# Small SBUF passes of VectorE moved to GpSimd and ScalarE, the first keys transposed by TensorE, and the stores issued from ScalarE

## The chip, the cores and the metric

The kernel runs on one core of one Trainium2 chip. The metric is the device time of one execution in microseconds, as the median of several runs. The core has five instruction streams: TensorE (PE, with its weight loads as PEld), VectorE (DVE), ScalarE (ACT), GpSimd (POOL) and SyncE (SP), which only issues DMAs here. Each stream runs in its own order and waits for the others by semaphores.

## The reference

Two layers follow one another. First an attention through 49 agents, with B = 4 batches of N = 11456 tokens of 128 channels:

```python
a2k = sm(agents, k)             # softmax over the tokens, 49 x N
agent_v = a2k @ v               # 49 x 128
q2a = sm(q, agents)             # softmax over the agents, N x 49
x = q2a @ agent_v               # N x 128
```

`sm` scales by 1/sqrt(128), subtracts the maximum, takes exp and divides by the sum. Then a mixture of 8 experts over all 45824 tokens, the best one for each:

```python
xn = x / (norm(x) + 1e-6); en = expert_emb / (norm(expert_emb) + 1e-6)
logits = xn @ en.T / tau
gate_w = softmax(logits)[argmax]
out[t] = gate_w * (relu(x[t] @ w1[e]) @ w2[e])      # e = argmax of token t, F = 1024
```

Inputs and output are fp32.

## The kernel before, in words

**Tiles.** A batch is cut into 12 units (`u`): eleven of 128 partitions x 8 token columns, and a last one of 96 x 2. Two tiles of 4 columns (512 tokens) make a unit; a batch has 23 tiles. Units are grouped for routing: group 0 is unit 0, and every later group two units.

**Stages of a batch.** (1) Key scores: each unit of `k` is transposed, multiplied with the agents, and a running maximum `m_run` is kept (`k1_unit`, `k1_f32`). (2) Value sums: `kd` = exp(scores - max), and `avp` = kd x v, added into `avx` (`k2_unit`). (3) `av_chain` divides, gives `avT`, and makes a small matrix `r_hi`, `r_lo` that yields in one product a token's logits, sum and quadratic form. (4) `pick_expert` guesses the batch's expert, loads its `w1` and `w2`, forms gh + gl = avT x w1 in two fp16 halves, and w2h + w2l. (5) Query units (`q_unit`): scores, exp, a split into `e` high and low halves, a transpose to `tt`, and the product `rtp` with r_hi, r_lo. (6) `route_group`: the gate `gs` of a group's tokens by some fifteen small passes over 128 x 16 or 128 x 16 x 8 numbers. (7) The expert steps: for each tile 8 steps of `ffn_mm1` (hp = gh x tt, L722 and L723, then ScalarE's relu `hh` L726 and VectorE's residual `hl` L727) and, four steps later, `ffn_mm2` (yp, L744 to L746); after eight steps `ffn_out` multiplies by the gate into `ot` (L759) and stores it (L765). There are 4 x 23 x 8 = 736 steps. (8) Tokens whose best expert is not the guessed one ("strays") are repaired in a late pass.

**fp16 split against fp32.** Most units are split into two fp16 halves (`split`: square and sum on ScalarE, a power-of-two scale in three tiny VectorE passes `half_scale`, the high half on ScalarE, the low half by two GpSimd passes L303 and L304), transposed by a DMA, and multiplied in three fp16 products. `pe_T` and `k1_f32` instead transpose in fp32 on TensorE (L364), copy the result out of PSUM (half on ScalarE, half on VectorE) and multiply in fp32 (L382). In the first batch the units 1, 3, 5 and 7 of `k` (`K16`) take a quick form of the split, with the low half on VectorE (L306) and the DMA transpose issued from ScalarE's queue (L309); the other eight are `k1_f32`.

**Order.** The program is written as generators that yield steps; `first` lists the work before the expert steps, with units of the next batch or of queries placed between the values by the table `BETWEEN`. During the expert steps `keys` spreads the next batch's units over the steps and `queries` starts each query unit some units ahead. A scheduler then orders each engine's instructions by a model of the machine; SyncE's order is kept as written in the first stage. PSUM has four banks for `hp`, two for `yp`, and two for scores and small products. Loads of k, q and v share eleven SBUF buffers (`ld`).

Until batch 0's gates' factor exists no expert step runs, so the program has a first stage (to the first L722) and then the expert stage, in which the next batch's keys and values and all queries run between the steps.

Of the kernel before, what the change touches and what calls it, by code (L numbers as in the profile page):

```python
# [30 lines left out]
def kernel(ctx: ExitStack, tc: tile.TileContext, q, k, v, agents, emb, tau, w1, w2, out):  # L31
# [141 lines left out]
    def half_scale(ssq, kexp, tag, bufs=2, fold=None):  # L173

        p = ssq.shape[0]
        sc = sm.tile([P, 1], F32, name="hsc", tag=tag + "c", bufs=bufs)[:p]
# [4 lines left out]
        dve.tensor_scalar(si, si, EXPONENT, None, ALU.bitwise_and)
        yield 1
        dve.tensor_scalar(iv.bitcast(I32), si, -1.0, float(254 * ONE), ALU.mult, ALU.add)
        if fold is not None:
            yield 1
            dve.tensor_scalar(iv, iv, fold[:p], None, ALU.mult)
# [104 lines left out]
    def split(kind, b, u, g, quick=False):  # L291
# [7 lines left out]
        hs = half_scale(sq, 14, kind + "u", 4, escale if kind == "q" else None)  # L299
        sc, iv = now_run(hs) if quick else (yield from hs)  # L300
        act.activation(xs[:p, :n, 0], s[:p, :n], AF.Copy, scale=sc)  # L301
        if not quick:
            pool.tensor_tensor(out=s[:p, :n], in0=s[:p, :n], in1=sc.unsqueeze(2).broadcast_to([p, n, D]), op=ALU.mult)  # L303
            pool.tensor_tensor(out=xs[:p, :n, 1], in0=s[:p, :n], in1=xs[:p, :n, 0], op=ALU.subtract)  # L304
# [4 lines left out]
        (act if quick else sp).dma_start_transpose(out=xT[:, : 2 * n, :p], in_=xs[:p, :n].rearrange("p c h d -> p (c h d)"))  # L309
# [62 lines left out]
    def k1_f32(b, u):  # L372
# [12 lines left out]
        act.activation(st, spv, AF.Copy, scale=sga[:p])  # L385
# [235 lines left out]
    def route_group(b, gi, n):  # L621
# [18 lines left out]

        pool.tensor_scalar(quad[:, :n], quad[:, :n], 1e-36, None, ALU.max)
# [1 line left out]
        dve.tensor_scalar(l.unsqueeze(2), rtg[:, :n, E:], 1e-9, None, ALU.add)
# [2 lines left out]
        pool.tensor_tensor(out=nrm, in0=quad[:, :n], in1=half[:, :n], op=ALU.pow)  # L646
# [21 lines left out]
        dve.scalar_tensor_tensor(out=el, in0=es, scalar=1e-9, in1=l, op0=ALU.add, op1=ALU.mult)  # L668
# [6 lines left out]
        dve.tensor_scalar(gs[:, :n], gs[:, :n], bt.iall, None, ALU.mult)  # L675
# [72 lines left out]
    def ffn_out(b, t):  # L748
# [16 lines left out]
        sp.dma_start(out=dst, in_=o[:p, :n])  # L765
# [364 lines left out]
```

## Time and profile before

| | |
|---|---|
| median of 3 runs | 1150.92 us (1150.88 to 1152.09) |
| the profiled execution | 1146.91 us, span 1145.1 us |
| first expert matmul (L722) | 121.84 us after the span's start |
| PE / DVE / ACT / POOL busy | 1031.5 / 866.8 / 712.7 / 515.4 us |
| mean granted TensorE clock | 0.947 |

Times are microseconds from the span's start. A row of the timeline is start, duration, engine, line, operation, output<-input, shapes and count, and in brackets how long the engine had idled and who released it. "SPq" and "ACTq" are DMA instructions on an engine's queue; they are not counted as busy. A row of the waits is: who waited for whom, the sum in us, how often, the longest. A row of the groups ends with busy us, mean ns of one | idle time before it and its releasers. The granted clock is the share of TensorE's full clock. Line numbers are those of the kernel before; in the changed one most are one or two off (L727 for L726, L728 for L727, L760 for L759, L766 for L765).

### The profile page before, as it was taken

What the parts mean: (1) busy time and instruction counts of PE and PEld (TensorE: products, weight loads), DVE (VectorE), ACT (ScalarE), POOL (GpSimd) and SP (SyncE); (2) the same over time, 40 slices, a digit from 0 to 9 for tenths busy, and PEclk for the clock granted to TensorE, in tenths of its full rate; (3) what the DMA queues carried; (4) which work ended last, traced back from release to release, by engine and by line L of the source; (5) the groups of instructions that cost most, each with busy time, mean ns of one, the idle gap of its engine ahead of it and who ended that gap; (6) DMA issues with size and microseconds to landing.
All of it is one profiled execution on the core that took longest, in us unless ns stands there. A gap on an engine that the chain in (4) does not pass through costs nothing.

```text
span 1145.1 us, 34081 instructions
## 1 busy us (share of the span) xinstructions
PE 1031.5 (90%) x13878; PEld 815.1 (71%) x13878; DVE 866.8 (76%) x2056; ACT 712.7 (62%) x1338; POOL 515.4 (45%) x449
## 2 busy tenths in 40 slices
PE   4677788999998888889999889999999799999997
PEld 4666566777777766667777667777778577887776
DVE  5446787877787778768688688877678889787785
ACT  4454967776657866756654876665455756655553
POOL 2262688756512986535430677354221624242100
PEclk9557899999999899999999899999999899999999
DMA  9959879953456997654433997733203534331100
GB/s 322 181 150 166 266 163 235 240 141 104 80 105 221 206 230 139 147 103 119 92 87 80 271 240 176 150 72 80 59 22 108 119 65 137 100 81 46 41 29 33
DMA packets 292264, 154.72 MB, mean 135 GB/s; under 512 B 216635, under 2 KB 268939, under 8 KB 292107
## 3 DMA queue, kind: packets, MB, share of 16 engines
q1 hardware_dynamic: 283723, 150.44, 54.9%
q10 hardware_dynamic: 8320, 2.10, 1.3%
q8 instruction: 109, 1.79, 0.6%
q14 instruction: 48, 0.39, 0.1%
q0 software_dynamic: 64, 0.00, 0.0%
HBM read 75.80 MB, written 23.53 MB: 87 GB/s over the span
## 4 chain that ended last, share of the span: by engine, by line
PE 53%; DMA 14%; issue 11%; DVE 9%; POOL 7%; ACT 4%; SPq 1%; ACTq 0%; POOLq 0%; DVEq 0%
PE hp L722 9%; PE yp L744 9%; PE yp L746 9%; PE yp L745 9%; PE hp L723 9%; PE avp L408 4%; DMA tt<-e 4%; DMA kt<-in_k_dram 3%; DVE hl L727 3%; DMA kT<-ks 2%; DMA qT<-qs 2%; POOL qt L303 2%; POOL kt L303 1%; POOL ks L304 1%; ACT hh L726 1%
## 5 line engine op out<-in xcount | busy, mean ns | idle before, releaser
L727 DVE SCALAR_TENSOR_TENSOR hl<-hp,hh 128x512 f16<-128x512 f32 (+1 forms) x736 | 479.6, 669 | 112.3 <-ACT hh L726 91.9
L726 ACT ACTIVATE hh<-hp 128x512 f16<-128x512 f32 (+1 forms) x736 | 416.5, 585 | 223.7 <-PE yp L745 132.4
L744 PE MATMUL yp<-w2h,hh 128*128 128x128 f16 (+1 forms) x2880 | 523.3, 220 | 6.4 <-ACT hh L726 6.2
L745 PE MATMUL yp<-w2l,hh 128*128 128x128 f16 (+1 forms) x2880 | 523.0, 220 | 2.7 <-DVE w2l L533 2.7
L746 PE MATMUL yp<-w2h,hl 128*128 128x128 f16 (+1 forms) x2880 | 522.4, 220 | 0.0
L744 PEld LDWEIGHTS <-hh 128*128 128x128 f16 (+1 forms) x2880 | 285.2, 99 | 61.5 <-ACT hh L726 8.5
L746 PEld LDWEIGHTS <-hl 128*128 128x128 f16 (+1 forms) x2880 | 285.6, 99 | 46.5 <-issue 3.9
L722 PE MATMUL hp<-tt,gh 128*128 128x512 f16 (+1 forms) x736 | 279.2, 379 | 40.0 <-DVE hl L727 35.3
L745 PEld LDWEIGHTS <-hh 128*128 128x128 f16 (+1 forms) x2880 | 285.2, 99 | 38.4 <-issue 0.3
L723 PE MATMUL hp<-tt,gl 128*128 128x512 f16 (+1 forms) x736 | 278.8, 379 | 0.0
L615 POOL TENSOR_TENSOR rt<-rt,qe 128x392 f32<-128x392 f32 (+1 forms) x48 | 46.3, 965 | 163.2 <-ACT rt L614 163.1
L303 POOL TENSOR_TENSOR qt<-qt,hsc 128x1024 f32<-128x1024 f32 (+1 forms) x46 | 81.9, 1783 | 66.2 <-ACT qs L301 52.8
L723 PEld LDWEIGHTS <-gl 128*128 128x128 f16 x736 | 72.5, 99 | 48.3 <-issue 46.3
L581 POOL TENSOR_TENSOR e<-qe,e 128x392 f16<-128x392 f32 (+1 forms) x48 | 41.5, 865 | 140.0 <-DVE e L580 62.9
L304 POOL TENSOR_TENSOR qs<-qt,qs 128x1024 f16<-128x1024 f32 (+1 forms) x46 | 93.1, 2027 | 0.6
L303 POOL TENSOR_TENSOR kt<-kt,hsc 128x1024 f32<-128x1024 f32 (+1 forms) x36 | 64.4, 1790 | 57.5 <-ACT ks L301 57.5
L722 PEld LDWEIGHTS <-gh 128*128 128x128 f16 x736 | 72.5, 98 | 10.0 <-issue 9.0
L304 POOL TENSOR_TENSOR ks<-kt,ks 128x1024 f16<-128x1024 f32 (+1 forms) x36 | 73.0, 2028 | 0.6
L759 DVE TENSOR_TENSOR ot<-yp,gs 128x512 f32<-128x512 f32 (+1 forms) x92 | 61.4, 668 | 14.5 <-PE yp L746 13.9
L646 POOL TENSOR_TENSOR nrm<-quad,half 128x16 f32<-128x16 f32 (+2 forms) x28 | 68.4, 2443 | 2.0
L408 PE MATMUL avp<-vt,kd 128*64 128x129 f32 x720 | 62.8, 298 | 5.1 <-ACT kd L402 4.8
L297 ACT ACTIVATE qs<-qt 128x1024 f16<-128x1024 f32 (+1 forms) x46 | 46.0, 1001 | 31.6 <-DMA qt<-in_q_dram 13.9
(258 smaller groups left out, 1483.7 us busy)
## 6 DMA issues: line engine op xcount, KB each, us to landing
kt<-in_k_dram SPq DMA_DIRECT2D x44, 512.0 KB, 6.0
qt<-in_q_dram SPq DMA_DIRECT2D x44, 512.0 KB, 7.0
vt<-in_v_dram SPq DMA_DIRECT2D x44, 512.0 KB, 5.4
out_dram<-ot SPq DMA_DIRECT2D x88, 256.0 KB, 2.2
w1s<-in_moe_w_dram SPq DMA_DIRECT2D x5, 512.0 KB, 3.6
w2s<-in_moe_w_dram SPq DMA_DIRECT2D x5, 512.0 KB, 4.9
qT<-qs SPq DMA_TRANSPOSE x46, 4.7
tt<-e SPq DMA_TRANSPOSE x46, 2.9
```

The lines of the kernel that those rows point to most:

```text
L303: pool.tensor_tensor(out=s[:p, :n], in0=s[:p, :n], in1=sc.unsqueeze(2).broadcast_to([p, n, D]), op=ALU.mult)
L304: pool.tensor_tensor(out=xs[:p, :n, 1], in0=s[:p, :n], in1=xs[:p, :n, 0], op=ALU.subtract)
L408: pe.matmul(out=avp[hs, :W], lhsT=de[:p, c * A : c * A + LO], rhs=src[:p, c, :], start=(c < 2), stop=(c >= n - 2), skip_group_check=True)
L646: pool.tensor_tensor(out=nrm, in0=quad[:, :n], in1=half[:, :n], op=ALU.pow)
L722: pe.matmul(out=hp[:, :m], lhsT=bt.gh[:, fs], rhs=tt, start=True, stop=False)
L723: pe.matmul(out=hp[:, :m], lhsT=bt.gl[:, fs], rhs=tt, start=False, stop=True)
L726: act.activation(hh[:, :m], hp[:, :m], AF.Relu)
L727: dve.scalar_tensor_tensor(out=hl[:, :m], in0=hp[:, :m], scalar=0.0, in1=hh[:, :m], op0=ALU.max, op1=ALU.subtract)
L744: pe.matmul(out=y, lhsT=hh[:, cs], rhs=bt.w2h[:, f, :], start=(f == 0 and c == 0), stop=False, skip_group_check=True)
L745: pe.matmul(out=y, lhsT=hh[:, cs], rhs=bt.w2l[:, f, :], start=False, stop=False, skip_group_check=True)
L746: pe.matmul(out=y, lhsT=hl[:, cs], rhs=bt.w2h[:, f, :], start=False, stop=last, skip_group_check=True)
L759: dve.tensor_tensor(out=o[:p, :n], in0=yp[:p, :n], in1=gate, op=ALU.mult)
```

## The change

Four things are changed.

1. All twelve units of batch 0's keys take `k1_f32`. The quick form of `split` is gone, and the scale of the scores is folded into the agents' power-of-two scale (`sga_s`). The table `BETWEEN` has four entries in place of seven: two query units and two key units of batch 1 (it had five keys).
2. In `route_group` the logits are no longer divided before their maximum is taken: the maximum is taken of the raw logits (`rmx`), subtracted, and then scaled. Additions, products and the subtraction go to GpSimd; the two reciprocals and the reductions stay on VectorE; the last product with `iall` goes to ScalarE. In `mark_strays` one addition, and for batches 1 to 3 the low half of `w2`, go to GpSimd.
3. The cast of `e` to its high half goes from VectorE to ScalarE; the query scale is folded into an integer bias (`qbias`) instead of a product; five products of one number a partition become `tensor_scalar` instead of `tensor_tensor`.
4. The output's stores are issued from ScalarE's queue.

```diff
-    def half_scale(ssq, kexp, tag, bufs=2, fold=None):
+    def half_scale(ssq, kexp, tag, bufs=2, bias=float(254 * ONE)):
...
-        dve.tensor_scalar(iv.bitcast(I32), si, -1.0, float(254 * ONE), ALU.mult, ALU.add)
-        if fold is not None:
-            yield 1
-            dve.tensor_scalar(iv, iv, fold[:p], None, ALU.mult)
+        dve.tensor_scalar(iv.bitcast(I32), si, -1.0, bias if isinstance(bias, float) else bias[:p], ALU.mult, ALU.add)
...
+    sga_s = cst.tile([P, 1], F32, name="sga_s")
+    dve.tensor_scalar(sga_s, sga, SCALE, None, ALU.mult)
     escale = cst.tile([P, 1], F32, name="escale")
-    dve.tensor_scalar(escale, isga, SCALE, None, ALU.mult)
+    dve.tensor_copy(escale, isga)
+    qbias = cst.tile([P, 1], F32, name="qbias")
+    dve.tensor_scalar(qbias, isga.bitcast(I32), float(127 * ONE), None, ALU.add)
...
-        if not quick:
-            pool.tensor_tensor(out=s[:p, :n], in0=s[:p, :n], in1=sc.unsqueeze(2).broadcast_to([p, n, D]), op=ALU.mult)
-            pool.tensor_tensor(out=xs[:p, :n, 1], in0=s[:p, :n], in1=xs[:p, :n, 0], op=ALU.subtract)
-        else:
-            dve.scalar_tensor_tensor(out=xs[:p, :n, 1], in0=s[:p, :n], scalar=sc, in1=xs[:p, :n, 0],
-                                     op0=ALU.mult, op1=ALU.subtract)
+        pool.tensor_tensor(out=s[:p, :n], in0=s[:p, :n], in1=sc.unsqueeze(2).broadcast_to([p, n, D]), op=ALU.mult)
+        pool.tensor_tensor(out=xs[:p, :n, 1], in0=s[:p, :n], in1=xs[:p, :n, 0], op=ALU.subtract)
...
-        (act if quick else sp).dma_start_transpose(out=xT[:, : 2 * n, :p], in_=xs[:p, :n].rearrange("p c h d -> p (c h d)"))
+        sp.dma_start_transpose(out=xT[:, : 2 * n, :p], in_=xs[:p, :n].rearrange("p c h d -> p (c h d)"))
...
-        dve.scalar_tensor_tensor(out=w2l, in0=w2s, scalar=s3, in1=w2h, op0=ALU.mult, op1=ALU.subtract)
+        if b == 0:
+            dve.scalar_tensor_tensor(out=w2l, in0=w2s, scalar=s3, in1=w2h, op0=ALU.mult, op1=ALU.subtract)
+        else:
+            pool.tensor_tensor(out=w2s, in0=w2s, in1=s3.unsqueeze(2).broadcast_to([P, NF, D]), op=ALU.mult)
+            pool.tensor_tensor(out=w2l, in0=w2s, in1=w2h, op=ALU.subtract)
...
-        dve.tensor_tensor(out=iall, in0=iall, in1=i3, op=ALU.mult)
+        dve.tensor_scalar(iall, iall, i3, None, ALU.mult)
...
-        dve.tensor_copy(hi, e)
-        pool.tensor_tensor(out=e2[:p, :n, LO : LO + A], in0=e, in1=hi, op=ALU.subtract)
+        act.copy(hi, e)
+        (dve if f32 else pool).tensor_tensor(out=e2[:p, :n, LO : LO + A], in0=e, in1=hi, op=ALU.subtract)
...
+        rmx = small("rmx")
+        dve.tensor_reduce(out=rmx, in_=rtg[:, :n, :E], axis=AX.X, op=ALU.max)
+
         pool.tensor_scalar(quad[:, :n], quad[:, :n], 1e-36, None, ALU.max)
-        l = small("l")
-        dve.tensor_scalar(l.unsqueeze(2), rtg[:, :n, E:], 1e-9, None, ALU.add)
-        yield 1
         nrm = small("nrm")
         pool.tensor_tensor(out=nrm, in0=quad[:, :n], in1=half[:, :n], op=ALU.pow)
+        l, ls = small("l"), small("ls")
+        pool.tensor_scalar(l.unsqueeze(2), rtg[:, :n, E:], 1e-9, None, ALU.add)
+        pool.tensor_tensor(out=ls, in0=l, in1=bt.sg6.broadcast_to([P, n]), op=ALU.mult)
+        pool.tensor_tensor(out=nrm, in0=ls, in1=nrm, op=ALU.add)
         yield 2
-        dve.scalar_tensor_tensor(out=nrm, in0=l, scalar=bt.sg6, in1=nrm, op0=ALU.mult, op1=ALU.add)
-        yield 1
+        lg = bt.lg[:, cols]
+        pool.tensor_tensor(out=lg, in0=rtg[:, :n, :E], in1=bc(rmx, E), op=ALU.subtract)
         cc = small("cc")
         dve.reciprocal(cc, nrm)
         yield 1
-        lg = bt.lg[:, cols]
-        dve.tensor_tensor(out=lg, in0=rtg[:, :n, :E], in1=bc(cc, E), op=ALU.mult)
-        yield 1
-        lmx = small("lmx")
-        dve.tensor_reduce(out=lmx, in_=lg, axis=AX.X, op=ALU.max)
-        yield 1
-        dve.tensor_tensor(out=lg, in0=lg, in1=bc(lmx, E), op=ALU.subtract)
+        pool.tensor_tensor(out=lg, in0=lg, in1=bc(cc, E), op=ALU.mult)
...
-        dve.scalar_tensor_tensor(out=el, in0=es, scalar=1e-9, in1=l, op0=ALU.add, op1=ALU.mult)
+        pool.tensor_scalar(el, es, 1e-9, None, ALU.add)
+        pool.tensor_tensor(out=el, in0=el, in1=l, op=ALU.mult)
...
-        dve.tensor_scalar(gs[:, :n], gs[:, :n], bt.iall, None, ALU.mult)
+        act.activation(gs[:, :n], gs[:, :n], AF.Copy, scale=bt.iall)
...
-        dve.tensor_tensor(out=oh, in0=oh, in1=iota8m.unsqueeze(1).broadcast_to([P, NCOL, E]), op=ALU.add)
+        pool.tensor_tensor(out=oh, in0=oh, in1=iota8m.unsqueeze(1).broadcast_to([P, NCOL, E]), op=ALU.add)
...
-        sp.dma_start(out=dst, in_=o[:p, :n])
+        act.dma_start(out=dst, in_=o[:p, :n])
...
-    K16 = (1, 3, 5, 7)
     QF = 2
-    BETWEEN = {2: ("k", 1, 0), 3: ("q", 0, 2), 4: ("k", 1, 1), 5: ("q", 0, 3), 6: ("k", 1, 2), 7: ("k", 1, 3), 8: ("k", 1, 4)}
+    BETWEEN = {1: ("q", 0, 2), 5: ("q", 0, 3), 8: ("k", 1, 0), 11: ("k", 1, 1)}
...
-                    spawn(k1_unit(b, u, (1, 4), True) if u in K16 else k1_f32(b, u))
+                    spawn(k1_f32(b, u))
```

More of the change, by code (lines that the diff above doesn't have):

```diff
@@ L198 @@
     sga, isga = now_run(pow2(now_run(allmax(amx, 1, "amxr", pss, 0)), 10, "sga"))
+    sga_s = cst.tile([P, 1], F32, name="sga_s")
+    dve.tensor_scalar(sga_s, sga, SCALE, None, ALU.mult)
     escale = cst.tile([P, 1], F32, name="escale")
-    dve.tensor_scalar(escale, isga, SCALE, None, ALU.mult)
+    dve.tensor_copy(escale, isga)
+    qbias = cst.tile([P, 1], F32, name="qbias")
+    dve.tensor_scalar(qbias, isga.bitcast(I32), float(127 * ONE), None, ALU.add)
     a16 = cst.tile([P, B, 2 * A], F16, name="a16")
-    act.activation(a16[:, :, :A], aT_all, AF.Copy, scale=sga)
-    dve.scalar_tensor_tensor(out=a16[:, :, A:], in0=aT_all, scalar=sga, in1=a16[:, :, :A], op0=ALU.mult, op1=ALU.subtract)
+    act.activation(a16[:, :, :A], aT_all, AF.Copy, scale=sga_s)
+    dve.scalar_tensor_tensor(out=a16[:, :, A:], in0=aT_all, scalar=sga_s, in1=a16[:, :, :A], op0=ALU.mult, op1=ALU.subtract)
     ones = cst.tile([P, P], F32, name="ones")
@@ L286, with split @@
     ready = []
-    def split(kind, b, u, g, quick=False):
+    def split(kind, b, u, g):
         s = units[kind, b, u]
@@ L298, in split @@
         yield g
-        hs = half_scale(sq, 14, kind + "u", 4, escale if kind == "q" else None)
-        sc, iv = now_run(hs) if quick else (yield from hs)
+        hs = half_scale(sq, 14, kind + "u", 4, *([qbias] if kind == "q" else []))
+        sc, iv = yield from hs
         act.activation(xs[:p, :n, 0], s[:p, :n], AF.Copy, scale=sc)
-        if not quick:
-            pool.tensor_tensor(out=s[:p, :n], in0=s[:p, :n], in1=sc.unsqueeze(2).broadcast_to([p, n, D]), op=ALU.mult)
-            pool.tensor_tensor(out=xs[:p, :n, 1], in0=s[:p, :n], in1=xs[:p, :n, 0], op=ALU.subtract)
-        else:
-            dve.scalar_tensor_tensor(out=xs[:p, :n, 1], in0=s[:p, :n], scalar=sc, in1=xs[:p, :n, 0],
-                                     op0=ALU.mult, op1=ALU.subtract)
+        pool.tensor_tensor(out=s[:p, :n], in0=s[:p, :n], in1=sc.unsqueeze(2).broadcast_to([p, n, D]), op=ALU.mult)
+        pool.tensor_tensor(out=xs[:p, :n, 1], in0=s[:p, :n], in1=xs[:p, :n, 0], op=ALU.subtract)
         xT = wk.tile([P, 2 * UJ, P], F16, name=kind + "T", tag="xT", bufs=XB)
-        (act if quick else sp).dma_start_transpose(out=xT[:, : 2 * n, :p], in_=xs[:p, :n].rearrange("p c h d -> p (c h d)"))
+        sp.dma_start_transpose(out=xT[:, : 2 * n, :p], in_=xs[:p, :n].rearrange("p c h d -> p (c h d)"))
         return xT, iv
@@ L341, in run_max, with k1_unit @@
             dve.scalar_tensor_tensor(out=mr, in0=spv, scalar=iv[:p], in1=mr, op0=ALU.mult, op1=ALU.max)
-    def k1_unit(b, u, g, quick=False):
+    def k1_unit(b, u, g):
         kb = blk_of(b, u)
@@ L347, in k1_unit @@
             yield 1
-        xT, iv = yield from split("k", b, u, g[0], quick)
+        xT, iv = yield from split("k", b, u, g[0])
         yield g[1]
@@ L384, in k1_f32 @@
         spv = s[:p, : n * A].rearrange("p (c a) -> p c a", a=A)
-        act.activation(st, spv, AF.Copy, scale=sga[:p])
-        run_max(kb, spv, sga, p, n)
+        act.activation(st, spv, AF.Copy, scale=sga_s[:p])
+        run_max(kb, spv, sga_s, p, n)
         kb.s[u] = st
@@ L455, in av_chain @@
         sg2 = sm.tile([P, 1], F32, name="sg2", tag="sg2")
-        dve.tensor_tensor(out=sg2, in0=bt.sg, in1=bt.sg, op=ALU.mult)
+        dve.tensor_scalar(sg2, bt.sg, bt.sg, None, ALU.mult)
         r_hi = sm.tile([P, RW], F16, name="r_hi", tag="r_hi")
@@ L515, in pick_expert @@
         sgw = sm.tile([P, 1], F32, name="sgw", tag="sgw")
-        dve.tensor_tensor(out=sgw, in0=s2, in1=bt.sg, op=ALU.mult)
+        dve.tensor_scalar(sgw, s2, bt.sg, None, ALU.mult)
         if b > 0:
@@ L536, in pick_expert @@
         iall = sm.tile([P, 1], F32, name="iall", tag="iall")
-        dve.tensor_tensor(out=iall, in0=bt.isg, in1=i2, op=ALU.mult)
+        dve.tensor_scalar(iall, bt.isg, i2, None, ALU.mult)
         yield 1
-        dve.tensor_tensor(out=iall, in0=iall, in1=i3, op=ALU.mult)
+        dve.tensor_scalar(iall, iall, i3, None, ALU.mult)
         bt.iall = iall
```

## The prediction

> **What bounds the kernel now.** I read the page's busy shares first, then the windows view cut at the stage borders, then the waits of TensorE, then the timelines of the places that the waits named.
>
> ```profile
> span 1145.1 us, 34081 instructions
> PE 1031.5 (90%) x13878; PEld 815.1 (71%) x13878; DVE 866.8 (76%) x2056; ACT 712.7 (62%) x1338; POOL 515.4 (45%) x449
> ...
> 7.60:12.80 5.20, 5.20 (x24) 4.62 (x24) 2.20 (x8) 3.37 (x5) 0.00 (x0) 1.00 1.02 418
> 12.80:19.40 6.60, 6.08 (x51) 5.39 (x49) 5.00 (x19) 4.80 (x11) 0.33 (x3) 1.00 1.04 382
> 19.40:26.60 7.20, 0.04 (x1) 0.00 (x0) 0.91 (x3) 0.30 (x2) 0.00 (x0) 0.75 1.17 276
> 26.60:50.30 23.70, 17.56 (x136) 16.00 (x136) 11.49 (x36) 9.71 (x18) 0.33 (x3) 0.50 1.16 185
> 80.40:105.90 25.50, 19.70 (x285) 16.70 (x285) 18.32 (x37) 12.27 (x20) 10.50 (x9) 0.80 0.96 155
> 121.80:1145.10 1023.30, 951.48 (x13119) 744.13 (x13116) 804.54 (x1875) 656.71 (x1241) 473.34 (x389) 0.98 0.53 126
> ```
>
> A window row gives its length, then the busy time of PE, PEld, DVE, ACT and POOL, the granted clock, the DMA share and GB/s. The program falls in two. From 121.8 on, the expert stage, TensorE is busy 951.5 of 1023.3 us at clock 0.98: it is the bound, and at most 71.8 us of idling can be won there. Before 121.8 no engine is the bound for long; TensorE sits still from 19.4 to 26.6 and then works at half clock. The start is a chain, and the next rows say of what.
>
> ```profile
> 18.10 8.40 ACTq L309 DMA_TRANSPOSE kT<-ks  x1
> ...
> 26.55 0.59 ACT L385 ACTIVATE s_u<-sp,p2s 128x392 f32<-128x392 f32 x1 [6.90 <-issue]
> ...
> 35.28 9.90 ACTq L309 DMA_TRANSPOSE kT<-ks  x1
> ...
> 45.23 0.59 ACT L352 ACTIVATE s_u<-sp,hiv 128x392 f32<-128x392 f32 x1 [9.01 <-issue]
> ```
>
> ScalarE's own queue is held 8.4 and 9.9 us by the issue of a DMA transpose, and the engine does nothing meanwhile (6.90 and 9.01 us idle, released by "issue"). What it should have done, emptying TensorE's score banks and copying transposed keys, is late by as much.
>
> For the expert stage the waits of TensorE, and the worst of them at 405 us:
>
> ```profile
> PE hp L722 <- DVE hl L727: 35.3, 33, 4.1
> PE rtp L598 <- DMA tt<-e: 9.8, 10, 3.2
> ...
> 403.11 2.12 POOL L304 TENSOR_TENSOR qs<-qt,qs 128x1024 f16<-128x1024 f32 x1
> 403.13 4.96 DVE L643 TENSOR_SCALAR l<-rtg 128x16 f32<-128x16 f32 x1
> 405.20 1.89 POOL L303 TENSOR_TENSOR qt<-qt,hsc 128x1024 f32<-128x1024 f32 x1
> 407.05 1.00 POOL L615 TENSOR_TENSOR rt<-rt,qe 128x392 f32<-128x392 f32 x1
> 408.48 1.27 DVE L727 SCALAR_TENSOR_TENSOR hl<-hp,hh 128x512 f16<-128x512 f32 x2
> 409.21 0.58 PE L722 MATMUL hp<-tt,gh 128*128 128x512 f16 x1 [4.11 <-DVE hl L727]
> ```
>
> An addition on 16 columns (L643) starts 0.02 us after a GpSimd pass and ends (408.09) as the third GpSimd pass in a row ends (408.05). The residual `hl` queued behind it on VectorE comes 5 us late, no bank of `hp` is free, and TensorE idles 4.11 us. So the largest wait of TensorE, 35.3 us, is in part VectorE held by GpSimd on small SBUF passes. How much, the groups and the spread of single durations tell (min/median/max):
>
> ```profile
> L643 DVE TENSOR_SCALAR l<-rtg 128x16 f32<-128x16 f32 (+2 forms) x28 | 21.3, 761 | 3.8 <-ACT rtg L613 3.8
> L675 DVE TENSOR_SCALAR gs<-gs,iall 128x16 f32<-128x16 f32 (+2 forms) x28 | 16.2, 577 | 0.3
> L668 DVE SCALAR_TENSOR_TENSOR el<-esa,l 128x16 f32<-128x16 f32 (+2 forms) x28 | 13.9, 498 | 0.5
> ...
> L643 DVE TENSOR_SCALAR l<-rtg x28: 154/174/4958, 116.7 to 1088.2; 128x16 f32<-128x16 f32 x20, 128x8 f32<-128x8 f32 x4, 128x2 f32<-128x2 f32 x4
> L675 DVE TENSOR_SCALAR gs<-gs,iall x28: 217/232/1861, 132.5 to 1097.1; 128x16 f32<-128x16 f32 x20, 128x8 f32<-128x8 f32 x4, 128x2 f32<-128x2 f32 x4
> L668 DVE SCALAR_TENSOR_TENSOR el<-esa,l x28: 152/174/1899, 131.8 to 1092.8; 128x16 f32<-128x16 f32 x20, 128x8 f32<-128x8 f32 x4, 128x2 f32<-128x2 f32 x4
> ```
>
> Mean less median, times 28: 16.4 + 9.7 + 9.1 = 35.2 us of holding in three lines of the seven that leave VectorE.
>
> **Part 1: the first keys.** The four DMA transposes on ScalarE go, with eight activations and four residuals; instead all 12 units of batch 0 pass TensorE in fp32, and the first query unit follows. The prices, at full and at half clock:
>
> ```profile
> 11.82 1.51 PE L364 MATMUL fTp<-ident,kt 128*128 128x128 f32 x8
> 14.09 1.99 PE L382 MATMUL sp<-aT_all,fT 128*128 128x49 f32 x16
> 28.57 3.49 PE L382 MATMUL sp<-aT_all,fT 128*128 128x49 f32 x16
> 36.27 1.12 PE L364 MATMUL fTp<-ident,kt 128*128 128x128 f32 x4 [0.93 <-ACT fT L369]
> 67.07 3.65 PE L564 MATMUL sp<-aT_all,fT 128*128 128x49 f32 x16 [0.70 <-DVE m_run L341]
> ```
>
> A transpose is 0.19 us at full clock (1.51/8), 0.28 at half (1.12/4); a score pass 0.124 (1.99/16) or 0.218 (3.49/16). Eleven units of 8 columns, one of 2 and the query unit make 98 transposes and 196 passes (two a product). Full clock: 18.6 + 24.3 = 42.9 us, from 7.6 to 50.5. Half: 27.4 + 42.7 = 70.1, to 77.7. Now the query scores end at 67.07 + 3.65 = 70.7. ScalarE and VectorE have per unit two passes of about 0.6 us each against TensorE's 3.5, so they hide. I take full clock with 5.5 us of waits, 56: a gain of 15, bounds -7 and +20. Full clock because the two windows from 7.6 to 19.4, this very work with little idling, have 1.00, and the half clock comes after a standstill.
>
> [...]
>
> From 70.7 to the end of the value sums (105.9) are 35.2 us. Of the seven units placed between the values, three keys of batch 1 go to the expert stage, with their transposes, and the clock there was 0.80 over 19.7 us busy: at 1.00 that alone is 4 us. I take 5, bounds 0 and 10. The chain from 105.9 to the first expert matmul at 121.8 hangs on the weights' load and stays. Start of the expert stage: 121.8 - 20 = 102 (bounds 129 and 92).
>
> Before, on ScalarE in this stage (fT are transposed keys copied out, ks the scaled halves, s_u the scores):
>
> ```order
> L369 COPY fT<-fTp 128x512
> L301 ACTIVATE ks<-kt,hsc 128x8x128
> L297 ACTIVATE ks,usq<-kt 128x8x128 x2
> L202 ACTIVATE a_128<-aT_all,p2s 128x4x49
> L385 ACTIVATE s_u<-sp,p2s 128x392
> L309 DMA_TRANSPOSE kT<-ks 128x16x128
> L385 ACTIVATE s_u<-sp,p2s 128x392
> ```
>
> And now, same engine and place:
>
> ```order
> L367 COPY fT<-fTp 128x512 x4
> L156 COPY pm<-mB 128x1
> L204 ACTIVATE a_132<-aT_all,sga_s 128x4x49
> L383 ACTIVATE s_u<-sp,sga_s 128x392
> L367 COPY fT<-fTp 128x512
> ```
>
> No transfer is issued between copies any more.
>
> **Part 2: the three key units moved.** TensorE pays their scores in the expert stage:
>
> ```profile
> L318 PE MATMUL sp<-a,kT 128*128 128x49 f16 (+1 forms) x302 | 34.5, 192 | 12.3 <-DMA kT<-ks 7.2 <-DVE hiv L186 5.1
> ```
>
> Three such lines, 302/8 = 38 units: at most 103/38 = 2.7 us a unit, less where the lines overlap. I take 4 us for three (bounds 0 and 8).
>
> **Part 3: VectorE's passes.** Seven more GpSimd passes a group (28 groups), the casts of `e` and the final gate product on ScalarE, one `hiv` product fewer per query unit. What the holding costs TensorE lies between 0 and the 35.3 us of the row above. I take 20, over half, as the longest of these waits (4.11) stands right behind a held pass. ScalarE pays 48 casts and 28 products; it idles 1023.3 - 656.7 = 366.6 us in this stage, which hides them, and I book 2 us for places where it is full.
>
> **Part 4: the gate chain on GpSimd.** Before, on VectorE, second group of batch 0 (es, el, gs lead to the gate, ot is the output tile):
>
> ```order
> L668 SCALAR_TENSOR_TENSOR el<-esa,l 128x16
> L617 TENSOR_REDUCE quad<-rt 128x8
> L727 SCALAR_TENSOR_TENSOR hl<-hp,hh 128x512
> L671 RECIPROCAL gs<-el 128x16
> L179 TENSOR_SCALAR hsc<-usq 128x1
> L727 SCALAR_TENSOR_TENSOR hl<-hp,hh 128x512
> L675 TENSOR_SCALAR gs<-gs,iall 128x16
> L181 TENSOR_SCALAR hsc<-hsc 128x1
> L727 SCALAR_TENSOR_TENSOR hl<-hp,hh 128x512 x2
> L759 TENSOR_TENSOR ot<-yp,gs 128x512
> ```
>
> Now on VectorE:
>
> ```order
> L728 SCALAR_TENSOR_TENSOR hl<-hp,hh 128x512
> L672 RECIPROCAL gs<-el 128x16
> L339 SCALAR_TENSOR_TENSOR m_run<-sp,hiv,m_run 128x392
> L760 TENSOR_TENSOR ot<-yp,gs 128x512 x2
> ```
>
> Two output tiles stand in a row: the gate comes so late that both output banks wait for it. Behind them wait TensorE's next output tile and all `hl` after it.
>
> ```profile
> 135.03 0.25 POOL L641 TENSOR_SCALAR quad<-quad 128x16 f32<-128x16 f32 x1 [0.89 <-DVE quad L617]
> 137.09 2.14 POOL L304 TENSOR_TENSOR qs<-qt,qs 128x1024 f16<-128x1024 f32 x1
> 139.18 2.94 POOL L646 TENSOR_TENSOR nrm<-quad,half 128x16 f32<-128x16 f32 x1
> 156.75 0.32 DVE L675 TENSOR_SCALAR gs<-gs,iall 128x16 f32<-128x16 f32 x1
> 168.69 0.68 DVE L759 TENSOR_TENSOR ot<-yp,gs 128x512 f32<-128x512 f32 x1
> ```
>
> In the new GpSimd order 8 first and 8 second splits of units, the power, two products, a remainder and seven small passes stand from `quad` to the last gate pass: 8 x 1.89 + 8 x 2.14 + 2.94 + 2.0 + 0.9 + 2 = 40 us. `quad` came 13.2 us after the stage began, so the gate comes 54 us after it, not 35. The first tile that needs it was written at +47. The two banks give a tile more; I take 5 us of TensorE idling over the three batch starts that have this (bounds 0 and 30).
>
> **Part 5: the stores.**
>
> ```profile
> L765 SPq DMA_DIRECT2D out_dram<-ot x92: 332/344/1436, 141.2 to 1139.4; - x92
> ...
> SPq L765 <- DVE ot L759: 220.9, 56, 10.4
> ```
>
> 92 issues of 0.34 us, 32 us in all, go to ScalarE, which waits there for `ot` with the next `hh` behind it. Four `hp` banks and the 366.6 us of ScalarE's idling cover it: 0. Above, +15, if ten stores take the 1.44 us where ScalarE is full. Below, -5: SyncE stood 220.9 us waiting for `ot` with loads and transposes queued behind the store, and half of TensorE's 9.8 us on transposed `tt` could go with that.
>
> **Sum** against the profiled execution (1146.9 us; span 1145.1 and 1.8 around it): 1146.9 - 15 - 5 + 4 - 20 + 2 + 5 + 0 = 1117.9. The median of the runs is 4.0 above the profiled one, so 1122.
>
> **Rivals.**
> R1, the start pays but the expert stage does not: new lateness on GpSimd and ScalarE eats what VectorE gains. 1150.9 - 20 + 4 + up to 10 = 1135 to 1145. For it: GpSimd is full in stretches already; against: VectorE loses work and holding both. 0.20.
> R2, half clock through the first keys: +7 in place of -15, no 5, the rest as forecast: 1122 + 27 = 1149, no change. 0.08.
> R3, slower: the gate chain on GpSimd (part 4). If GpSimd is also kept waiting inside the chain, TensorE loses the whole 54 - 35 = 19 us at three starts: 1122 + 57 - 5 = 1174. It decides from 11 us a start (34 in all). Against it: pace before was 47 us for three tiles, so much of the 19 is slack. 0.13.
> R4, both pay fully (VectorE's 35, the start 30): 1122 - 25 = 1097. 0.07.
> Forecast: 0.52, own range 1108 to 1136.
>
> Range 1100 to 1152 leaves R3 and part of R4. A measurement here tells 0.2%, 2.3 us, from no change. Faster: the forecast, R1, R4 and little of R2, 0.80; same 0.05; slower 0.15.
>
> **What would show it.** Right: first `hp` near 102 us and clock 1.00 from about 10 to 50; ACT with no 8 us "issue" wait; no pass of `l`, `el`, `gs` over 1 us on VectorE; "hp <- DVE hl" near 15 us. Wrong: the first `hp` after 115; TensorE waiting on `ot`, or GpSimd busy without a break for 40 us while `gs` is awaited; ScalarE idle at L766.

## The result and the profile after

| | before | after |
|---|---|---|
| median of the runs | 1150.9 us (1147.7 to 1152.1, 4 runs) | 1105.1 us (1101.6 to 1110.3, 4 runs) |
| profiled execution, and its span | 1146.9, 1145.1 us | 1101.6, 1099.8 us |
| first expert matmul | 121.8 us | 101.2 us |
| expert stage (from there to the end of the span) | 1023.3 us | 998.6 us |

The ratio is 0.961, 95% interval 0.957 to 0.965: faster, by 45.8 us. Of the 45.3 us that the span lost, 20.6 lie in the start and 24.7 in the expert stage. The forecast was 102 for the first expert matmul and a stage 9 us shorter.

The page of the changed kernel, its span, the shares of busy time and the granted clock in 40 slices:

```profile
span 1099.8 us, 33877 instructions
PE 1019.3 (93%) x13878; PEld 809.8 (74%) x13878; DVE 770.5 (70%) x1779; ACT 724.2 (66%) x1406; POOL 580.1 (53%) x653
...
PEclk9777999999999999999999999999999999999999
```

VectorE lost 96 us of work, ScalarE and GpSimd took 11.5 and 65. The windows of the changed kernel, cut at its own stage borders (length, busy time of PE, PEld, DVE, ACT, POOL, clock, DMA share, GB/s):

```profile
7.60:39.40 31.80, 30.26 (x248) 29.33 (x247) 19.72 (x51) 15.55 (x29) 4.97 (x11) 1.00 0.97 315
39.40:50.30 10.90, 10.20 (x52) 9.89 (x52) 4.33 (x12) 2.64 (x5) 4.01 (x2) 0.55 0.40 110
50.30:84.00 33.70, 23.91 (x249) 21.55 (x248) 20.90 (x40) 16.80 (x28) 9.69 (x8) 0.69 0.37 87
84.00:101.20 17.20, 9.82 (x121) 7.79 (x121) 7.31 (x34) 8.10 (x20) 4.83 (x9) 0.70 0.94 256
101.20:1099.80 998.60, 944.46 (x13216) 740.77 (x13212) 711.78 (x1628) 679.79 (x1325) 550.76 (x597) 0.99 0.57 132
```

The query scores end at 50.3, the value sums at 84.0 (70.7 and 105.9 before). In the first window TensorE works through transposes and scores almost without a break. Eight transposes take 1.97 us at its start and 1.05 us at 35.05: up to 13.2 us TensorE runs at half the later pace, though the view gives 1.00 there too (the trace has no record of the clock before 13.3 us, and the view counts that as full). ScalarE, up to 101 us, has no wait for "issue" among its ten largest, of which one is shown:

```profile
7.66 1.97 PE L362 MATMUL fTp<-ident,kt 128*128 128x128 f32 x8
...
35.05 1.05 PE L362 MATMUL fTp<-ident,qt 128*128 128x128 f32 x8
...
ACT s_u L383 <- PE sp L380: 14.5, 11, 2.5
```

In the expert stage TensorE's idle time fell from 71.8 to 54.1 us (998.6 less 944.5), and its busy time from 951.5 to 944.5, though it has three more key units to do there: its clock there is 0.99, not 0.98. Added up over the matmuls that took over 1.4 times the median of their kind, the time lost to half clock in this stage was 19.7 us and is 10.1.

TensorE's waits in the changed kernel (us in all, times, longest):

```profile
PE hp L723 <- DVE hl L728: 21.2, 34, 5.0
PE rtp L600 <- DMA tt<-e: 11.4, 14, 2.2
...
PE yp L745 <- DVE ot L760: 0.9, 2, 0.6
```

The wait for `hl` fell from 35.3 to 21.2 us, not to 15; output tiles cost 0.9 us. The durations (min, median, max) of two of the passes that left VectorE:

```profile
L650 POOL TENSOR_SCALAR l<-rtg x28: 222/266/1142, 96.4 to 1041.7; 128x16 f32<-128x16 f32 x20, 128x8 f32<-128x8 f32 x4, 128x2 f32<-128x2 f32 x4
L676 ACT ACTIVATE gs<-gs,iall x28: 291/302/390, 115.9 to 1046.7; 128x16 f32<-128x16 f32 x20, 128x8 f32<-128x8 f32 x4, 128x2 f32<-128x2 f32 x4
```

Nowhere do they last the 5 us that `l` took on VectorE. All that VectorE's passes took above the median of their kind (where over 0.1 us) added up to 66.5 us before and 6.6 now, over the whole span.

### The profile page after: what moved, and what is told of

The parts are those of the page before. It is cut to its first block, busy times and chain, and to the rows that moved or that the text cites. A ratio compares the mean times of both kernels' runs of the same rounds, so it can differ in the third digit from the quotient of the medians.

```text
span 1099.8 us, 33877 instructions
## 1 busy us (share of the span) xinstructions
PE 1019.3 (93%) x13878; PEld 809.8 (74%) x13878; DVE 770.5 (70%) x1779; ACT 724.2 (66%) x1406; POOL 580.1 (53%) x653
## 4 chain that ended last, share of the span: by engine, by line
PE 53%; DMA 13%; POOL 13%; issue 9%; ACT 6%; DVE 5%; SPq 1%; ACTq 0%; POOLq 0%; DVEq 0%
PE hp L723 9%; PE yp L745 8%; PE yp L747 8%; PE hp L724 8%; PE yp L746 8%; DMA kT<-ks 4%; DMA tt<-e 4%; PE avp L406 4%; DMA qt<-in_q_dram 3%; POOL qs L305 2%; POOL qt L304 2%; POOL ks L305 2%; ACT hh L727 2%; POOL kt L304 2%; PE sp L380 2%
## 5 line engine op out<-in xcount | busy, mean ns | idle before, releaser
L723 PE MATMUL hp<-tt,gh 128*128 128x512 f16 (+1 forms) x736 | 275.9, 375 | 22.4 <-DVE hl L728 21.2
L724 PE MATMUL hp<-tt,gl 128*128 128x512 f16 (+1 forms) x736 | 276.0, 375 | 0.0
L304 POOL TENSOR_TENSOR qt<-qt,hsc 128x1024 f32<-128x1024 f32 (+1 forms) x46 | 81.8, 1781 | 49.6 <-ACT qs L303 42.9
L650 POOL TENSOR_SCALAR l<-rtg 128x16 f32<-128x16 f32 (+2 forms) x28 | 8.2, 293 | 133.1 <-ACT rtg L615 132.4
```

Of the source, the lines that this page charges most:

```text
L723: pe.matmul(out=hp[:, :m], lhsT=bt.gh[:, fs], rhs=tt, start=True, stop=False)
L724: pe.matmul(out=hp[:, :m], lhsT=bt.gl[:, fs], rhs=tt, start=False, stop=True)
```

## The experiments

Each was timed against the kernel before, with its ratio and 95% interval; "stage" is the expert stage of its profiled execution. A stage varies for reasons that are nobody's edit: the runs of one kernel lie up to 9 us apart (1101.6 to 1110.3 above), and runs 9 and 11 below have stages 7.3 us apart with the same order of instructions in their traces but for four stores on ScalarE. A difference of stages under some 8 us is therefore put down to no part. The kernel before had a median of 1150.9 us above and of 1146.1 to 1148.0 beside the experiments, so a few microseconds between runs are read with the ratios beside them.

**1. The old start with everything else new.**

```diff
+    K16 = (1, 3, 5, 7)
...
-    BETWEEN = {1: ("q", 0, 2), 5: ("q", 0, 3), 8: ("k", 1, 0), 11: ("k", 1, 1)}
+    BETWEEN = {2: ("k", 1, 0), 3: ("q", 0, 2), 4: ("k", 1, 1), 5: ("q", 0, 3), 6: ("k", 1, 2), 7: ("k", 1, 3), 8: ("k", 1, 4)}
...
-                    spawn(k1_f32(b, u))
+                    spawn(k1_unit(b, u, (1, 4), True) if u in K16 else k1_f32(b, u))
```

(with the quick path of `split` as before.)

> The changed kernel with the start of the kernel before (four key units by DMA transposes on ScalarE's queue, the seven old entries between the values); the expert stage keeps everything new. Theory A (start and expert stage are two separate gains): the first expert matmul is back near 122 us, the expert stage stays near 999 us long, so 1121 to 1128 us, about 20 above the changed kernel. Rival B (the expert stage gained because of what the new start hands over, fewer key units and another order of loads): the stage goes back to 1010 to 1023 us and the time to 1135 to 1150.

1120.4 us, ratio 0.976 (0.973 to 0.979). First expert matmul at 119.5, stage 997.9. Theory A holds, B falls: the expert stage keeps its whole gain without the new start. In the changed kernel the three key units moved into the stage cost nothing that can be seen (998.6 against 997.9).

**2. The gate passes back on VectorE.** `l`, `nrm`, both `lga`, `el` and `gs` as in the kernel before; cast, w2l, stores and start new.

```diff
-        pool.tensor_scalar(el, es, 1e-9, None, ALU.add)
-        pool.tensor_tensor(out=el, in0=el, in1=l, op=ALU.mult)
+        dve.scalar_tensor_tensor(out=el, in0=es, scalar=1e-9, in1=l, op0=ALU.add, op1=ALU.mult)
...
-        act.activation(gs[:, :n], gs[:, :n], AF.Copy, scale=bt.iall)
+        dve.tensor_scalar(gs[:, :n], gs[:, :n], bt.iall, None, ALU.mult)
```

> The changed kernel with the small gate passes of a group (l, nrm, lga, el, gs) on VectorE as before; the start, the stores, the cast of e and w2l stay new. Theory A (VectorE held by GpSimd on these passes cost TensorE its waits and, behind the long ones, stretches at half clock): single passes of 1.3 to 5 us on L-lines of l, el, gs, lga come back, 40 to 60 us of them in all, TensorE waits over 30 us for hl against 21.2, the half-clock stretches of the expert stage grow from 10 us of lost time to 15 to 20, and the time is 1120 to 1130 us. Rival C (the stores on ScalarE's queue, or VectorE's casts, made the gain): no more than 1108 us.

1119.7 us, ratio 0.975 (0.973 to 0.977). One of VectorE's groups in this run, and its expert stage:

```profile
L677 DVE TENSOR_SCALAR gs<-gs,iall 128x16 f32<-128x16 f32 (+2 forms) x28 | 21.0, 749 | 0.5
...
101.40:1119.20 1017.80, 949.18 (x13215) 743.47 (x13211) 780.91 (x1795) 676.41 (x1297) 502.04 (x405) 0.98 0.56 129
```

The long passes are back (0.75 us in the mean for `gs`, 0.23 undisturbed), 41.7 us of them above the median, and the stage is 19.2 us longer. The direct wait for `hl` rose only to 23.9 us, under the 30 expected; the rest went to the scalings `hiv` (6.9) and `hsc` (3.3) and `w2l` (2.6), which stand in the same queue, and the half-clock loss rose to 14.2. C falls.

**3. The stores back on SyncE.**

```diff
-        act.dma_start(out=dst, in_=o[:p, :n])
+        sp.dma_start(out=dst, in_=o[:p, :n])
```

> The changed kernel with the stores of the output issued by SyncE as before. Theory A: the stores are worth nothing either way, 1103 to 1108 us. Rival C (stores that wait for ot in SyncE's queue hold up the loads and transposes behind them, and this was the expert stage's gain): TensorE's waits for tt and kT grow from 11.4 and 3.5 us to 25 or more, ScalarE's for qT and kT too, and the time is 1115 to 1130 us.

1105.2 us, ratio 0.962 (0.960 to 0.964), against 1105.1 of the changed kernel. The wait for `tt` rose to 18.5 us and that for `hl` fell to 12.3. The stores are worth nothing that these runs can tell; C falls. The expert stage of its profiled execution, which was the slowest of its four runs (1109.7 us):

```profile
101.60:1107.90 1006.30, 952.43 (x13215) 745.19 (x13211) 712.68 (x1628) 681.06 (x1325) 551.19 (x597) 0.98 0.56 131
```

TensorE idles as long as in the changed kernel (53.9 against 54.1 us) and is busy 8 us longer.

**4. The cast of `e` back on VectorE.**

```diff
-        act.copy(hi, e)
-        (dve if f32 else pool).tensor_tensor(out=e2[:p, :n, LO : LO + A], in0=e, in1=hi, op=ALU.subtract)
+        dve.tensor_copy(hi, e)
+        pool.tensor_tensor(out=e2[:p, :n, LO : LO + A], in0=e, in1=hi, op=ALU.subtract)
```

> The changed kernel with the cast of e on VectorE as before (its passes were held 8.6 us in all before). Theory A: 3 to 8 us slower than the changed kernel, 1108 to 1113, TensorE's waits for VectorE 3 us or more longer, passes of the cast up to 2.2 us. Rival E (ScalarE is as full as VectorE there, and the cast's place is indifferent): 1103 to 1107.

1125.6 us, ratio 0.981 (0.975 to 0.986): 20 us slower than the changed kernel, more than either theory allowed. Its expert stage, waits, the cast's durations (min, median, max) and two places of its timeline:

```profile
99.00:1127.10 1028.10, 955.70 (x13215) 749.18 (x13211) 739.35 (x1670) 667.73 (x1282) 553.84 (x598) 0.98 0.55 128
...
PE hp L723 <- DVE hl L728: 30.3, 36, 3.4
PE rtp L600 <- DMA tt<-e: 22.8, 9, 7.8
...
L582 DVE CAST e<-qe x48: 201/362/3447, 52.2 to 1061.7; 128x392 f16<-128x392 f32 x44, 96x98 f16<-96x98 f32 x4
...
155.78 3.28 SPq L307 DMA_TRANSPOSE kT<-ks  x1
159.16 1.25 SPq L591 DMA_TRANSPOSE tt<-e  x1
...
371.63 3.44 DVE L582 CAST e<-qe 128x392 f16<-128x392 f32 x1
372.67 2.13 POOL L305 TENSOR_TENSOR ks<-kt,ks 128x1024 f16<-128x1024 f32 x1
```

A cast is now held for 3.44 us, with `hl` behind it (TensorE idles 3.38 us from 372.1). But the holding adds up to only 15 us over 14 casts; of the 29.5 us of the stage, 9 are more waiting for `hl`, 11.4 more for `tt`, and 9.8 more half clock (19.9 against 10.1). The longest wait for `tt`, 7.8 us, comes from SyncE's queue: the transpose to `tt`, whose input GpSimd has ready at 156.0, is begun at 159.16 behind a transpose of keys. Which part of that is the cast, and which the order of issue that came with it, is open.

**5. The cast alone, in the kernel before.**

```diff
-        dve.tensor_copy(hi, e)
+        act.copy(hi, e)
```

> The kernel before with one line changed: the cast of e to fp16 on ScalarE, not on VectorE. Putting it back in the changed kernel cost 20 us. Theory R (the cast alone does it: held by GpSimd, it delays hl and, before the transposes, tt): 10 to 20 us of gain here too, 1127 to 1137 us, the stage 1003 to 1013. Rival S (the cast pays only where the gate passes have left VectorE as well): within 5 us of the kernel before, 1141 to 1148.

1144.3 us, ratio 0.998 (0.995 to 1.001), stage 1021.8 against 1023.3. R falls, S holds: the same line that is worth 20 us in the changed kernel is worth 0.2% in the one before, which the interval does not tell from nothing. TensorE waits as long for `hl` as before (34.9 against 35.3 us); that it does so because the gate passes are still held on VectorE fits, and is not shown by itself.

**6. The new start alone, in the kernel before.**

```diff
-    K16 = (1, 3, 5, 7)
+    K16 = ()
...
-    BETWEEN = {2: ("k", 1, 0), 3: ("q", 0, 2), 4: ("k", 1, 1), 5: ("q", 0, 3), 6: ("k", 1, 2), 7: ("k", 1, 3), 8: ("k", 1, 4)}
+    BETWEEN = {1: ("q", 0, 2), 5: ("q", 0, 3), 8: ("k", 1, 0), 11: ("k", 1, 1)}
```

> The kernel before with the new start alone (all first keys by TensorE in fp32, the four new entries between the values); gate, casts, w2l and stores as before. Theory A: first expert matmul at 101 to 104 us, expert stage 1023 to 1027 us (1023.3 before, and up to 4 for three more key units in it), 1127 to 1132 us. Against the run with the gate alone put back (stage 1017.8 us) it tells what the casts, w2l and the stores give together: 5 to 9 us. Rival B (the new start helps the expert stage): stage below 1015 us, time below 1120.

1140.3 us, ratio 0.995 (0.992 to 0.997). The first expert matmul is at 101.3 as expected, but the stage takes 1038.6 us, 15.3 more than before. Neither theory had that.

**7. The new keys, but the old seven entries**, to tell why.

```diff
-    K16 = (1, 3, 5, 7)
+    K16 = ()
```

> The kernel before with all first keys by TensorE in fp32, and its seven old entries between the values kept (five key units of batch 1 in the start, not two). The run with the new start alone had an expert stage of 1038.6 us, 15.3 longer than before. Theory P (the three key units moved into the expert stage cost it those 15 us, since VectorE and GpSimd are short there): stage back to 1019 to 1027 us, first expert matmul at 102 to 110, 1126 to 1134 us. Rival Q (the stage is longer for another reason, for example an order that happens to be worse): stage 1034 to 1042, 1138 us or more.

1121.2 us, ratio 0.976 (0.971 to 0.981). The stages of runs 6 and 7, with the two largest waits of TensorE:

```profile
101.30:1139.90 1038.60, 954.11 (x13210) 746.54 (x13209) 809.39 (x1887) 664.55 (x1252) 485.23 (x395) 0.98 0.54 127
...
PE hp L722 <- DVE hl L727: 35.0, 31, 4.8
PE rtp L598 <- DMA tt<-e: 19.9, 15, 3.1
```

```profile
98.50:1121.10 1022.60, 948.22 (x13121) 742.23 (x13117) 804.10 (x1877) 657.94 (x1241) 474.39 (x389) 0.98 0.52 126
...
PE hp L722 <- DVE hl L727: 33.8, 35, 4.1
PE rtp L598 <- DMA tt<-e: 12.5, 12, 2.6
```

P holds for the stage: with the key units back in the start it is as long as before. The new keys alone are worth 27 us; with the first expert matmul at 98.5, earlier than the 102 to 110 expected, the time lies 5 us below P's range. Three key units more in the stage cost 16 us there, 7 of them as a longer wait for `tt`, while VectorE is held; run 1 against the changed kernel shows no cost of them once it is not.

**8. As many passes on VectorE, but none that is held.**

```diff
+        jk = small("jk")
+        dve.reciprocal(jk, half[:, :n])
...
+        dve.tensor_reduce(out=jk, in_=rtg[:, :n, :E], axis=AX.X, op=ALU.max)
```

The reciprocal stands four times, where `l`, `nrm`, `el` and `gs` were, the reduction twice, where `lga` was.

> The changed kernel, with six passes a group put on VectorE in place of the six that left it, but of the kinds that no row shows held by GpSimd (four reciprocals of 128x16, two reductions of 128x16x8; their results are not used). VectorE's own work is then as with the gate passes on it, about 40 us in all. Theory A1 (the run with the gate on VectorE lost 14.6 us by the holding: 41.7 us of passes above their median): TensorE's stage stays within 4 us of 998.6, 1103 to 1109 us. Rival A2 (it lost them because VectorE had more passes to do between two hl, held or not): 1114 to 1121 us, as that run (1119.7).

1112.8 us, ratio 0.972 (0.967 to 0.976), between the two theories. Its stage, with 2 us of passes above their median in it, so that none was held:

```profile
101.30:1107.60 1006.30, 950.85 (x13215) 743.98 (x13212) 732.65 (x1784) 680.97 (x1325) 551.68 (x597) 0.98 0.56 131
```

By the medians, 7.7 of the 14.6 us of run 2 come from VectorE having more to do and 6.9 from the holding; by the ratios it is 12 of 16, with intervals that overlap run 2's. But 6.4 of the 7.7 us by which this stage is longer are busy time of TensorE, which run 3, with no pass added, has even more of. TensorE's idling tells more: 55.4 us here, 54.1 in the changed kernel, 68.6 in run 2. So in these executions the waits that run 2 adds come with the holding and not with the number of passes; the split of the whole time is not settled.

**9. The embeddings' norm on GpSimd.** The changed kernel's clock falls at 40.6 us. Ahead of that stand, on VectorE, GpSimd and TensorE:

```profile
34.67 1.89 POOL L304 TENSOR_TENSOR qt<-qt,hsc 128x1024 f32<-128x1024 f32 x1 [1.02 <-ACT qs L303]
34.75 1.82 DVE L238 SCALAR_TENSOR_TENSOR tr<-tr,xc 8x1 f32<-8x1 f32 x1
36.64 2.12 POOL L305 TENSOR_TENSOR qs<-qt,qs 128x1024 f16<-128x1024 f32 x1
36.79 1.99 DVE L242 TENSOR_TENSOR emb_n<-xc,yr 8x1 f32<-8x1 f32 x1
38.70 0.61 DVE L339 SCALAR_TENSOR_TENSOR m_run<-sp,sga_s,m_run 128x392 f32<-128x392 f32 x1
39.37 6.60 PE L380 MATMUL sp<-aT_all,fT 128*128 128x49 f32 x36 [1.54 <-DVE m_run L339]
```

Two passes over 8 numbers last as long as the GpSimd passes beside them, the running maximum is late, and TensorE idles 1.54 us.

```diff
-        yield from sqrt_into(emb_n, emb_n, E, 1, "en")
+        pool.tensor_scalar(emb_n, emb_n, 1e-36, None, ALU.max)
+        pool.tensor_tensor(out=emb_n, in0=emb_n, in1=half[:E, :1], op=ALU.pow)
+        yield 12
```

> The changed kernel with the norm of the expert embeddings (13 passes of VectorE over 8x1 numbers) taken by two GpSimd passes (max, power). In the changed kernel two of those 8x1 passes take 1.82 and 1.99 us at 34.75 and 36.79 us, while GpSimd splits a query unit; the running maximum behind them is late, TensorE idles 1.54 us and its clock is 0.50 from 42 to 64 us. Theory A (the same holding by GpSimd makes this stall, and the stall the half clock): no such pass, no idling there, clock 1.00 on to about 46 us, where the query scores end (50.3 now), the first expert matmul 4 to 10 us earlier than 101.2, time 1095 to 1101. Rival D (the clock falls there for another reason, or the start is set by the loads of the values): first expert matmul at 100 to 102, 1103 to 1107 us.

1100.7 us, ratio 0.958 (0.954 to 0.961), whose interval overlaps that of the changed kernel. The first expert matmul is at 97.9, so the edit was worth 3.3 us of the start (the stall itself was 1.54); but the clock falls at 41.3 all the same, with no idling ahead of it. That half of theory A falls.

**10. Transposes among the last scores.** On top of run 9, one 128x128 transpose behind each score product of the last four key units and of the first two query units: 34 up to the end of the first query unit's scores, and the second query unit's eight, which the expectation counts but does not name, from 54 us on.

```diff
+            if u >= NU - 4:
+                pe.transpose(out=wt[:p, :P], in_=kT[:, c * p : (c + 1) * p], identity=ident)
...
+                pe.transpose(out=wt[:p, :P], in_=xT[:, c * p : (c + 1) * p], identity=ident)
```

> The run with the embeddings' norm on GpSimd, and 42 transposes of 128x128 more on TensorE, one behind each score product of the last four key units and of the first query unit; their results are not used, and they take 4.6 us at full clock. In that run the clock fell to half at 41.2 us though TensorE had not idled since 7.6: since 36.2 it did nothing but score products of 49 columns. Theory F (a stretch of nothing but 49-column products loses the full clock): clock 1.00 past 41 us to the end of the query scores, near 47 to 48 us in spite of the added work, 1098 to 1102 us. Rival G (the clock falls after about 34 us of full work whatever it is, or by another timer): half clock from about 41 us on all the same, query scores end at 52 to 54, 1103 to 1108 us.

1106.4 us, ratio 0.963 (0.958 to 0.969). Windows of run 9, and then of this run:

```profile
36.30:38.70 2.40, 2.40 (x24) 2.40 (x23) 1.06 (x2) 0.85 (x3) 2.37 (x3) 1.00 0.77 229
38.70:41.10 2.40, 2.40 (x24) 2.40 (x23) 1.71 (x5) 2.24 (x5) 0.44 (x2) 1.00 1.09 288
41.30:43.20 1.90, 1.26 (x8) 1.10 (x7) 0.62 (x1) 1.17 (x3) 1.58 (x1) 0.50 0.69 183
```

```profile
41.10:44.40 3.30, 3.30 (x33) 3.22 (x32) 1.29 (x4) 2.29 (x4) 2.09 (x3) 1.00 0.78 198
44.40:46.90 2.50, 2.50 (x24) 2.34 (x23) 1.69 (x4) 0.22 (x1) 1.99 (x1) 1.00 0.68 188
47.00:49.80 2.80, 0.00 (x0) 0.00 (x0) 1.55 (x3) 1.06 (x2) 0.00 (x0) 1.00 0.68 197
50.90:59.00 8.10, 7.08 (x38) 6.28 (x38) 6.51 (x9) 4.41 (x9) 4.45 (x4) 0.50 0.26 69
```

F holds for the clock: with transposes among the 49-column products it stays at 1.00 to the end of the query scores, 47.0 us, which is where they end in run 9 (46.9) without the 34 transposes (3.7 us, at the 0.109 us from one start to the next). Then TensorE idles 2.9 us for the softmax of the first query unit and the clock falls at 50.7. The first expert matmul is at 97.1, against 97.9 in run 9, and the time lies where G had put it: next to nothing is won.

**11. The second query unit's scores into that idle time**, on top of run 9.

```diff
-                g = q_unit(b, u, (0, 1, 0, 0, 1, 0) if u < QF else (1, 6, 1, 1, 5, 1))
+                g = q_unit(b, u, (0, 1, 3, 0, 1, 0) if u < QF else (1, 6, 1, 1, 5, 1))
```

> The run with the embeddings' norm on GpSimd, with the second query unit's transposes and scores ahead of the first one's fp16 transposes on TensorE (they follow them now, while TensorE idles 3.05 us for the first unit's softmax). Theory T (the chain of the start is TensorE's order here): no idling of 3 us there, first expert matmul at 93 to 96 us against 97.9, 1095 to 1099 us. Rival U (the values and their sums set the rest of the start): 97 to 99 us, 1099 to 1102.

1087.7 us, ratio 0.949 (0.943 to 0.955): the fastest version, below the changed kernel's interval. TensorE in the start of this run:

```profile
42.42 5.78 PE L568 MATMUL sp<-aT_all,fT 128*128 128x49 f32 x26 [1.00 <-DVE m_run L341]
48.00 0.41 PE L149 MATMUL mT<-ident,m 128*49 128x128 f32 x1
48.21 1.36 PE L568 MATMUL sp<-aT_all,fT 128*128 128x49 f32 x6
49.49 0.66 PE L154 MATMUL mB<-ident,mTx 49*128 49x49 f32 x2
50.09 1.04 PE L590 MATMUL tp<-ident,e 128*128 128x128 f16 x8
```

The 3 us of idling are gone, and the first expert matmul is at 91.1, 6.8 us earlier than in run 9. Theory T holds, and more. The medians differ by 13 us, though the stage, 993.0 against 1000.3 us, has the same order of instructions in both but for four stores. Of the 7.3 us, 6.3 are a shorter wait for `hl` (14.0 against 20.3); why it is shorter is not shown.

**12. `rtp` three steps later**, on top of run 11.

```diff
-                spawn(q_unit(b, u, (1, 7, 1, 1, 6, 2)), 3)
+                spawn(q_unit(b, u, (1, 7, 1, 1, 9, 2)), 3)
```

> As the run with the second query unit early, and the product rtp of a query unit put three steps later behind its DMA transpose (9 steps, not 6). TensorE waits 11 to 23 us for tt in all runs. Theory V (that wait is only an order too tight by a few us): under 5 us of it left, expert stage 988 to 995 us, 1085 to 1094 us. Rival W (the wait moves on: the gate comes later, output tiles wait for it, or hl takes its place): stage 996 to 1004, 1094 to 1101.

1099.1 us, ratio 0.956 (0.950 to 0.962): 11 us slower than run 11 (their runs lie at 1092.3 to 1100.4 and 1084.1 to 1093.0). The wait for `tt` fell only from 15.1 to 11.1 us, that for `hh` rose from 7.4 to 11.1, one of 2.3 for `ot` came, and the half-clock loss rose from 12.6 to 19.8. V falls, W holds, at a stage of 1007.9.

## Why the prediction was right, and where not

The sign, and the range, were right. The gain was 45.8 us, not 29, and the time lies below the 1108 to 1136 that the forecast named as its own range. By its own steps:

- **Start, 102: measured 101.2.** Right in sum by luck, for the terms were off both ways. The query scores end at 50.3, not 56. A transpose was priced at 0.19 us from a row of eight (1.51 us from 11.82 on) in the midst of which TensorE's pace doubled: transposes start 0.21 us apart up to 12.7 us, and 0.11 us apart from there on. So the two windows from 7.6 to 19.4 were not both at full clock, as was read from their 1.00; in the changed kernel full clock held from 13.3 to 40.6 us. Counted with half pace up to 13.2, the work at full clock is some 33 us (5.60 us at half, 24.66 at 1.00, 10.20 at 0.55), not 42.9. The value stage then gave 1.5 us (35.2 to 33.7), not 5, and the last leg, taken as unchanged, grew from 15.9 to 17.2.
- **Three key units, +4:** wrong both ways, as one price. In the new stage they cost no more than can be told from nothing (0.7 us, run 1), in the old one 16 (runs 6 and 7).
- **VectorE held, -20, and ScalarE +2:** mis-sized. The wait for `hl` fell by 14.1 us, TensorE's whole idle time by 17.7. That the gate passes and the cast carry the gain is shown (runs 2 and 4); that the holding makes the waits is borne out by the idling (run 8), while how much of the whole time is the holding's is open. And the terms do not add: gate alone back 14.6, cast alone back 20.5, the cast alone in the kernel before 3.5 of 1147.9 (run 5).
- **Half clock behind the waits: not in the sum at all.** The busy time of TensorE was taken as given, plus 4; between the two profiled executions it fell by 7.0, as 9.6 us less were lost to half clock, so that the stage's 24.7 are 17.7 of idling and 7.0 of this. That the change brought the 7.0 is not shown: 18.7 us are lost to half clock in run 3 and 19.8 in run 12, in which VectorE is relieved too, and 19.7 in the kernel before. The idling does tell the versions apart: 50.7 to 62.8 us in the eight in which gate passes and cast have both left VectorE, 68.6 to 84.5 in the six others.
- **Gate late, +5, and R3:** the lateness was right, its price not. The gate of the second group comes at 160.5 us, 59 after the stage's beginning (54 forecast, 35 before), GpSimd is busy 39.3 of the 39.6 us ahead of it, and two output tiles follow in a row, at 160.5 and 161.1. Yet TensorE waits only 0.6 us for `ot` there: of the first four output tiles only the third is later than before (59 us after the stage's beginning, not 47), the fourth is written at 60 and was at 62.
- **Stores, 0:** right (run 3).
- **From profiled to median, +4.0:** measured 3.5.

R1 (nothing back in the expert stage) and R2 (half clock through the first keys) fell; R4 (start 30, VectorE's 35) came nearer in sum, 54 us against 45.8, with both parts too large: the start gave 20.6 and the wait for `hl` 14.1. Of the signs named, first `hp` near 102, no long "issue" wait on ScalarE, and no long passes of `l`, `el`, `gs` on VectorE came true; clock 1.00 from about 10 to 50 held from 13.3 to 40.6; "hp <- DVE hl" is 21.2, not near 15. One sign of being wrong came true without being one: GpSimd without a break for 40 us while `gs` is awaited.

## What to carry to other kernels

Price a stall of the bounding engine with what its clock loses behind it (4.2 us at half clock behind one of 4.97 us in the changed kernel), and do not add the prices of edits that relieve one queue: here one line was worth 3.5 us (its interval reaches to none) or 20, and three units of work nothing or 16, depending on whether the other edits were in. Look for what still stands idle on the chain of the start before filling it with anything: an order that moved ready work into 3 us of idling gave more than keeping the clock up did.
